# Loads of the first five units and of both weights, split in halves between the SP queue and the ScalarE queue

## The chip, the cores and the metric

One core of a Trainium2 chip runs the whole kernel. The metric is the device time of one execution in microseconds (us). On one core a single run's state is not marked by a second die, so runs more than 1.5% above the fastest of the same kernel are taken as slow and left out of the ratios. Times in the tables are medians; times of single instructions come from the profiled execution of each kernel, counted from the start of its span.

## The reference, cut to what matters

The program is a recurrent attention (a state of 48x48 per head that decays by w and takes in k times v), followed by a feed-forward block with a SoLU activation and a layer norm.

```python
def _attn_ref(r, k, v, w, u):            # batch 4, heads 8, sequence 768, head size 48
    for t in range(S):
        cur = einsum('bhd,bhe->bhde', u[None] * kt, vt)
        y[:, :, t] = einsum('bhd,bhde->bhe', rt, state + cur)
        state = wt[:, :, :, None] * state + einsum('bhd,bhe->bhde', kt, vt)

def _moe_ref(x, w_in, w_out, g_ln):      # 3072 tokens, 384 -> 1024 -> 384
    h = x @ w_in
    solu = h * softmax(h)                # [written out in the reference]
    return layernorm(solu) * g_ln @ w_out
```

All inputs and the output are float32.

## The kernel before

The work is cut into 24 units of 128 time steps of one batch. A unit needs four tensors, w, k, r and v, of 128 x 8 x 48 float32 (192 KB, 1,024 rows of 192 bytes). All loads are issued by SyncE, the SP queue. Those of units 0 to 4 and of both weights are asked for at the very start:

```python
    def load(i):
        c, b = units[i]
        for name, src in (("w", w), ("k", k), ("r", r), ("v", v)):
            t = io.tile([C, H, D], F32, tag=name + "_in", name=name + "_in")      # 6 buffers
            sp.dma_start(out=t, in_=src[b, :, c * C:(c + 1) * C, :].rearrange("h t d -> t h d"))
            live[i][name] = t

    # [u and g rows: two small loads from sp]
    load(0)
    win_f = consts.tile([128, KM, DF], F32)
    sp.dma_start(out=win_f, in_=moe_w_in.rearrange("(ko ki) f -> ki ko f", ki=128))
    load(1)
    # [w_out: two halves, both from sp]
    for i in range(2, 5):
        load(i)
```

ScalarE ("act") opens each unit with the logarithm of w; the running sums, the decays and all else hang on it:

```python
    def log_w(i):
        act.activation(out=L["lw"][:, :, :D], in_=L["w"], func=LN)
    def decays(i):
        act.activation(out=cum[:, :, :DM], in_=cum[:, :, :DM], func=EXP)
```

A fixed list of stages gives the order of instructions on every engine, and each engine keeps that order:

```python
ORDER = """
lw0 cum0 vb0 p0 win1 rows ubc exp0 q0 kp0 p1 rp0 lw1 cum1 dg0 win2 win0 exp1 kp1 krk1 ... gw3 M0 ...
lw2 ... lw3 ...
mean m2 mean_sb sel2 kp3 et0 H0 e0 p3 rp3 H1 Y2 lw4 q3 w2 he0 krk3 krr3 y2 Oa0 ...
"""                                                          # [cut]
```

The stages "win" cast w_in to bf16, "gw" scale w_out, "mean" and "w2" centre it, "H" is the first matmul of the feed-forward block, and "Oa0" is the first half of the output matmuls of unit 0.

The softmax here doesn't subtract the row's maximum and nothing guards it: scores larger than these inputs give would overflow.

## Time and profile before

| | before |
|---|---|
| device time, median of the first 3 runs | 170.99 us (169.93 to 172.01) |
| span of the profiled run | 169.6 us |
| TensorE, VectorE, ScalarE, GpSimd busy | 85%, 71%, 70%, 63% |
| first activation on ScalarE | 4.60 us |
| first output matmul | 37.30 us |
| loads of the start | 7.08 MB |

Read it as two stages. Until the first output matmul TensorE is idle for half of the time (18.8 of 37.3 us): it waits for data and for a string of short steps on the other engines. After it TensorE is almost never idle. The lines that show this stand in the prediction.

### The profile page before, as it was taken

How to read it: one execution, taken by the hardware profiler on the slowest of the kernel's cores; microseconds unless marked ns; L12 is line 12 of the kernel's file. 1: busy time of each engine (PE TensorE's matmuls, PEld its weight loads, DVE VectorE, ACT ScalarE, POOL GpSimd, SP SyncE). 2: the span in 40 equal slices, each digit the busy share in tenths (PEclk: the TensorE clock that was granted, in tenths of full speed). 3: DMA queues.
4: the chain of work that ended last, by engine and by line, in shares of the span. 5: the costliest groups of instructions: out<-in, count | busy, mean ns of one | idle time of the engine just before them, and what ended most of it. 6: DMA issues, size and time to landing. Idle time of an engine off the chain costs nothing.

```text
span 169.6 us, 5377 instructions
## 1 busy us (share of the span) xinstructions
PE 144.7 (85%) x2139; PEld 114.4 (67%) x2139; DVE 119.8 (71%) x280; ACT 118.2 (70%) x243; POOL 107.4 (63%) x157
## 2 busy tenths in 40 slices
PE   0503669939899999999999999999999999999980
PEld 0102336816788798878878887788877778798860
DVE  7017577796978779778988867697767988665440
ACT  3305395534869878888788968987878786767752
POOL 3225595824899886969989955779365629544000
PEclk9999999987999999999999999999999999999996
DMA  3999999999999999899999998999921011101212
GB/s 78 249 320 224 325 179 192 167 190 187 170 203 182 203 176 213 199 199 178 240 183 183 178 243 165 192 183 163 249 90 50 0 50 46 50 2 50 93 48 93
DMA packets 104795, 27.09 MB, mean 160 GB/s; under 512 B 100281, under 2 KB 104386, under 8 KB 104770
## 3 DMA queue, kind: packets, MB, share of 16 engines
q1 hardware_dynamic: 104770, 26.75, 79.7%
q8 instruction: 16, 0.26, 0.7%
q14 instruction: 9, 0.07, 0.1%
HBM read 22.03 MB, written 4.72 MB: 158 GB/s over the span
## 4 chain that ended last, share of the span: by engine, by line
PE 78%; DVE 6%; DMA 5%; ACT 3%; SPq 2%; POOL 2%; issue 2%; POOLq 0%; DVEq 0%
PE o_ps L63 22%; PE h_ps L63 18%; PE kr_ps L63 7%; PE g_ps L63 6%; PE y_ps L63 6%; PE m_ps L63 5%; PE s_ps L63 5%; DMA w_in<-in_w_dram 5%; PE cum_ps L63 4%; PE x_ps L63 3%; DVE w L63 3%; SPq L63 2%; POOL m L63 1%; DVE kr L63 1%; PE mean_ps L63 1%
## 5 line engine op out<-in xcount | busy, mean ns | idle before, releaser
L63 PE MATMUL o_ps<-w,he 128*128 128x385 bf16 x192 | 51.8, 330 | 2.9 <-DVE he L63 2.9
L63 PE MATMUL g_ps<-he 128*128 128x128 bf16 x192 | 42.3, 221 | 0.0
L63 POOL TENSOR_SCALAR_AFFINE_SELECT m<-m 128x1024 bf16<-128x1024 bf16 x24 | 26.4, 1101 | 18.9 <-ACT m L63 14.5
L63 PE MATMUL h_ps<-xT,win_sb 128*128 128x128 bf16 x576 | 35.9, 219 | 0.0
L63 PEld LDWEIGHTS <-win_sb 128*128 128x128 bf16 x576 | 32.8, 98 | 0.8 <-DVE xT L63 0.5
L63 PE MATMUL o_ps<-inv_col,e 128*128 128x1 bf16 x192 | 32.2, 168 | 0.0
L63 ACT ACTIVATE e<-h_ps 128x1024 bf16<-128x1024 f32 x24 | 24.5, 1022 | 9.8 <-PE h_ps L63 9.8
L63 DVE TENSOR_TENSOR he<-h_ps,e 128x1024 bf16<-128x1024 f32 x24 | 29.3, 1223 | 2.2 <-ACT e L63 1.3
L63 ACT CAST m<-m_ps 128x1024 bf16<-128x1024 f32 x24 | 24.3, 1012 | 8.9 <-PE m_ps L63 8.6
L63 PEld LDWEIGHTS <-he 128*128 128x128 bf16 x384 | 24.5, 97 | 4.9 <-DVE he L63 3.1
L63 PEld LDWEIGHTS <-e 128*128 128x128 bf16 x192 | 18.8, 98 | 13.3 <-issue 0.9
L63 POOL TENSOR_TENSOR dv<-vb,dg 128x384 bf16<-128x384 bf16 x24 | 19.8, 828 | 10.1 <-DVE dg L63 10.0
L63 POOL TENSOR_TENSOR q<-p,u_bc 128x384 bf16<-128x384 bf16 x24 | 21.8, 910 | 4.7 <-DVE gr L63 4.2
L63 POOL TENSOR_TENSOR p<-r_in,k_in 128x384 bf16<-128x384 f32 x24 | 24.1, 1003 | 1.0 <-DMA r_in<-in_r_dram 1.0
L63 DVE COPY kr<-kr_ps 128x1024 bf16<-128x1024 bf16 x24 | 16.5, 690 | 10.2 <-PE kr_ps L63 10.0
L63 ACT ACTIVATE cum_ps<-cum_ps 128x768 f32<-128x768 f32 x24 | 19.2, 801 | 5.2 <-PE cum_ps L63 3.0
L63 ACT ACTIVATE lw<-w_in 128x384 bf16<-128x384 f32 x23 | 12.0, 522 | 7.1 <-DMA w_in<-in_w_dram 7.1
L63 DVE TENSOR_TENSOR kp<-cum_ps,k_in 128x384 bf16<-128x384 f32 x24 | 13.4, 556 | 4.8 <-ACT cum_ps L63 4.0
L63 PEld LDWEIGHTS <-kr 64*128 64x128 bf16 (+1 forms) x272 | 11.5, 99 | 6.3 <-DVE kr L63 2.8
L63 POOL TENSOR_TENSOR qm<-ss,sq 128x1 f32<-128x1 f32 x24 | 4.5, 189 | 17.2 <-DVE junk L63 13.7
L63 DVE TENSOR_TENSOR st<-s_ps,et 64x192 bf16<-64x192 f32 x40 | 14.1, 352 | 1.6 <-ACT et L63 0.6
L63 ACT ACTIVATE o<-o_ps,rs 128x384 f32<-128x384 f32 x24 | 13.9, 579 | 0.3
(72 smaller groups left out, 253.4 us busy)
## 6 DMA issues: line engine op xcount, KB each, us to landing
w_in<-in_w_dram SPq DMA_DIRECT2D x24, 192.0 KB, 4.6
k_in<-in_k_dram SPq DMA_DIRECT2D x24, 192.0 KB, 4.6
r_in<-in_r_dram SPq DMA_DIRECT2D x24, 192.0 KB, 4.8
v_in<-in_v_dram SPq DMA_DIRECT2D x24, 192.0 KB, 4.8
out_dram<-o SPq DMA_DIRECT2D x24, 192.0 KB, 2.9
win_f<-in_moe_w_in_dram SPq DMA_DIRECT2D x1, 1536.0 KB, 8.1
wout_f<-in_moe_w_out_dram SPq DMA_DIRECT2D x2, 768.0 KB, 7.0
u_row<-in_u_dram SPq DMA_DIRECT2D x1, 1.5 KB
```

What stands on the lines that cost most here:

```text
L63: made = make(*args, **kwargs)
```

## The change

The intent is to have two queues ask for the data of the start. Each tensor of units 0 to 4, w_in and w_out becomes two halves, one from SP and one from ScalarE's queue. Units 5 to 23 stay whole and on SP.

```diff
         for name, src in (("w", w), ("k", k), ("r", r), ("v", v)):
             t = io.tile([C, H, D], F32, tag=name + "_in", name=name + "_in")
-            sp.dma_start(out=t, in_=src[b, :, c * C:(c + 1) * C, :].rearrange("h t d -> t h d"))
+            rows = src[b, :, c * C:(c + 1) * C, :].rearrange("h t d -> t h d")
+            if i < 5:
+                sp.dma_start(out=t[:, :H // 2, :], in_=rows[:, :H // 2, :])
+                act.dma_start(out=t[:, H // 2:, :], in_=rows[:, H // 2:, :])
+            else:
+                sp.dma_start(out=t, in_=rows)
@@
-    sp.dma_start(out=win_f, in_=moe_w_in.rearrange("(ko ki) f -> ki ko f", ki=128))
+    win_v = moe_w_in.rearrange("(ko ki) f -> ki ko f", ki=128)
+    for half, queue in enumerate((sp, act)):
+        part = slice(half * DF // 2, (half + 1) * DF // 2)
+        queue.dma_start(out=win_f[:, :, part], in_=win_v[:, :, part])
@@
-    for half in range(2):
+    for half, queue in enumerate((sp, act)):
         part = slice(half * KF // 2, (half + 1) * KF // 2)
-        sp.dma_start(out=wout_f[:, part, :], in_=wout_v[:, part, :])
+        queue.dma_start(out=wout_f[:, part, :], in_=wout_v[:, part, :])
```

## The prediction

> **What bounds the kernel now.** I began with the page's busy shares and its 40 slices (4.24 us each). TensorE is busy 85% of the span, the others 63 to 71%, and the slices show two stages. The last row is the mean busy share of the 16 DMA engines.
>
> ```profile
> PE   0503669939899999999999999999999999999980
> DMA  3999999999999999899999998999921011101212
> ```
>
> TensorE is nearly full from the ninth or tenth slice to the last but one; before that it is mostly idle. The DMA engines are full from the second slice to the 29th. The view of stretches puts numbers on it (columns: stretch, length, TensorE busy, instructions, granted clock, DMA share, GB/s):
>
> ```profile
> 0.00:37.30 37.30, 18.47 (x172) 1.00 1.02 215
> ...
> 40.00:165.00 125.00, 123.56 (x1947) 1.00 0.75 146
> ```
>
> From 40 to 165 us TensorE does 123.56 us of work in 125 us. Nothing but fewer or quicker matmuls shortens that stage. The other 37 us are the start, and any gain from loads must come from there: 18.47 us of TensorE work in 37.3 us, 18.8 us idle. The end of the start is in the chain of waits, in order of time (start, length, what):
>
> ```profile
> 31.42 4.69 DVE w L63 x8
> 36.11 1.14 DVE he L63
> 37.26 0.05 issue
> 37.30 0.50 PE o_ps L63
> ```
>
> At 37.30 the first output matmuls begin, and TensorE is dense from there. So the measure of the change is: when do these matmuls begin? The timeline of ScalarE shows what holds the start back now:
>
> ```profile
> 4.60 0.52 ACT L60 ACTIVATE lw<-w_in 128x384 bf16<-128x384 f32 x1 [2.51 <-DMA w_in<-in_w_dram]
> 6.00 0.80 ACT L63 ACTIVATE cum_ps<-cum_ps 128x768 f32<-128x768 f32 x1 [0.89 <-PE cum_ps L63]
> 13.34 0.52 ACT L63 ACTIVATE lw<-w_in 128x384 bf16<-128x384 f32 x1 [6.54 <-DMA w_in<-in_w_dram]
> ...
> 19.27 0.61 ACT L63 ACTIVATE gw<-wout_f,gr 128x384 bf16<-128x384 f32 x1 [3.73 <-DMA wout_f<-in_moe_w_out_dram]
> ```
>
> ScalarE works on unit 0 at 4.60 us, then waits 6.54 us for the data of unit 1, which queue behind the 1.5 MB of w_in. These are the waits that the change is aimed at. But they are waits for bytes, not for the queue that asks for them: in 0 to 37.3 us the DMA share is 1.02.
>
> The timeline of the SP queue shows the price of asking (start, length of the issue):
>
> ```profile
> 5.33 0.49 SPq L63 DMA_DIRECT2D w_in<-in_w_dram  x1
> 5.86 2.08 SPq L63 DMA_DIRECT2D k_in<-in_k_dram  x1
> 7.98 3.98 SPq L63 DMA_DIRECT2D r_in<-in_r_dram  x1
> ...
> 27.93 2.01 SPq L63 DMA_DIRECT2D r_in<-in_r_dram  x1
> 29.98 0.79 SPq L63 DMA_DIRECT2D v_in<-in_v_dram  x1
> ```
>
> An issue with room ahead of it takes about 0.4 to 0.5 us; the third one after w_in takes 3.98 us, because the transfers ahead have not drained. The last of the start's loads (v of unit 4) is issued only at 29.98 to 30.77 us. SP has nothing else to do, so this costs nothing today. That is the row to remember.
>
> **What the Trainium skill says.** "DMA: Bandwidth & Descriptors", section "Issuing engines are not separate DMA queues": DMAs begun by ScalarE and SyncE run on the same 16 DMA engines and interleave; several issuers save only the issue time. The trace agrees as far as it can: the share is 1.02 with one issuer. Same page, "Queues, rings and completion order": SP and ACT each own one row, with a ring on each engine. So I expect ACT to have its own depth ahead; no row of this trace shows ACT issuing. "Perfetto Trace Analysis", section "DMA Instruction — HWDGE (DVE, Sync)": the reported length runs from the semaphores being satisfied until the sequencer is free for its next instruction, and includes the wait for the shared descriptor generator. The SP rows agree: each issue starts 0.04 us after the last ended. "TensorE: Matmul & The Clock Gate", section "Architectural detail": ScalarE's queue is a strict FIFO. So an activation cannot pass a DMA issue written ahead of it.
>
> **The change part by part.**
> *Removed:* half the bytes of each of 20 unit loads and of w_in from SP. w_out already was two halves; its second one moves to ACT.
> *Added:* 22 issues on ACT (5 units x 4, one half each of w_in and w_out). The order of instructions of the changed kernel shows all 22 after the table load and ahead of the first activation (lw of unit 0). PE, VectorE and GpSimd keep their order and work. Bytes are the same: 20 x 196,608 + 2 x 1,572,864 = 7.08 MB.
>
> *When ACT is free.* v loads land a median 4.3 us after their issue starts (0 to 36 us), so today v of unit 4 lands at 29.98 + 4.3 = 34.3 us. With the engines already full I keep that time. Its issue ended at 30.77, so one queue can stand 34.3 - 30.77 = 3.5 us ahead of the data, some 3.4 tensors at about 1.03 us each. Two rings of that depth, drained evenly, hold twice that, 7.1 us: ACT's last issue ends at 34.3 - 7.1 = 27.2 us. If the depth is shared, at 30.8. I choose **27.5 us** for the first activation, against 4.60.
>
> *What follows it.* All first-unit data are there by then, so I lay the rows of the trace after t0 (start of the first activation). Today exp of unit 0 starts 1.40 after lw (6.00 - 4.60) and takes 0.80: t0+2.2. lw of unit 1 takes 0.52. TensorE's order puts the u and g transposes (1.65 + 0.27 us, ending about t0+3.2) ahead of unit 1's cumulation, 0.8 us: t0+4.0. Then exp of unit 1, 0.80, to t0+4.85, and VectorE, meanwhile through its copies, kp, rp and a reduction of unit 0, starts kp of unit 1 at about t0+5.2. Today that row starts at 15.58, and the output matmuls 21.7 us later (37.30). That stretch is a string of dependent short steps and the 4.69 us of w2 sums, so it moves nearly whole. What it loses is the wait for w_out: gw at 19.27 to 19.88 pushed the copy of m, whose matmuls were done at 19.05, to 19.79, 0.7 us. So the output matmuls start at t0 + 5.2 + 21.7 - 0.7 = t0 + 26.2 = 53.7 us, against 37.3: **16.4 us later**.
>
> *What comes back.* Nothing that I can see. TensorE has the same work left at that point and was 98.8% busy doing it (123.56 of 125). Loads from unit 5 on are SP's alone and run ahead of need: DMA is nearly idle after the 29th slice. The sum is 171.0 + 16.4 = **187.4 us**.
>
> **The rivals.**
> *ACT's issues do not block it* (it hands them off, or its ring is far deeper). The start would be bounded by bytes as before: lw of unit 0 maybe 0.3 us sooner, w_in at 12.3 us about the same. Time 170 to 171, the same. Against it: SP issues visibly stall up to 3.98 us, and ACT needs more than 20 issues, where one queue stood only 3.4 tensors ahead.
> *Two rings draw more bandwidth.* Unit loads run at some 180 GB/s while the stretch of 5 to 12 us with w_in in it reached 306, so 192-byte rows leave speed unused. If two rings gave a fifth more, the loads would land near 28 us, ACT be free at about 22, and the time be 171.0 + 22 - 11.1 = 182. For it: that 306. Against: the share is 1.0 already. To beat 171 ACT would have to be free by 11.1 us, which means nearly all 7.08 MB gone by then; impossible at these rates.
> *The depth is one for both, or the queues wait for each other's lock.* ACT free at 31: 171 + 31 - 11.1 = 191.
> *The delay is absorbed later.* It would need idle TensorE time after 37.3 us; there are 1.4 us in 125.
>
> **Range and chances.** Time = 171.0 + t0 - 11.1. t0 from 22 to 31.5 us gives 182 to 191.5, with half a us for the rest of the string on either side. Slower by over 2% needs only t0 above 14.5 us; the chance that it fails is that of the first rival, some 5%.
>
> **What would show it.** In ScalarE's timeline: no activation before some 27 us. In ACT's issues: 22 of them, the first few under 0.6 us, later ones stalled like SP's. Output matmuls near 53.7. DMA share about 1 with about 215 GB/s in the first 30 us, loads landing near 34. TensorE idle some 35 us before the dense stage, which stays as dense. It is wrong if an activation stands among the issues, if the loads land well before 30 us, or if the stretch from unit 1's kp to the output matmuls is not about 21 us.

## The result and the profile after

The changed kernel takes 188.31 us (median of 4 runs, 187.69 to 188.78), against 171.25 us before (4 runs, 169.93 to 172.01). The ratio is 1.1003, with a 95% interval of 1.0925 to 1.1081. Here and below a ratio is the mean time of one kernel's fast runs over that of the other's of the same rounds, so it is not quite the ratio of the medians quoted.

The two rows of the 40 slices, each now 4.64 us, in the page of the changed kernel:

```profile
PE   0000006579758999999999999999999999999990
DMA  6999999999830699699939899777960102101122
```

TensorE now does nothing in the first six slices. The DMA engines were full from the second slice, as before: the data came, and hardly anybody worked on them. In the view of stretches (stretch, length, then busy time of TensorE, its weight loads, VectorE, ScalarE and GpSimd, granted clock, DMA share, GB/s):

```profile
0.00:53.20 53.20, 17.09 (x173) 11.30 (x173) 22.98 (x68) 16.35 (x26) 19.21 (x32) 1.00 1.21 208
...
56.00:181.00 125.00, 123.69 (x1941) 101.09 (x1939) 95.29 (x207) 99.26 (x212) 87.35 (x123) 0.99 0.62 125
```

The start grew from 37.3 to 53.2 us with the same TensorE work in it (18.47 and 17.09 us, busy). The dense stage is as dense as it was: 123.69 us of 125, before 123.56. So nearly the whole difference lies ahead of the first output matmul: 15.9 us of the 16.1 by which the two profiled spans differ (169.6 and 185.7 us). The chain of waits, in order of time:

```profile
52.00 1.14 DVE he L63
53.14 0.05 issue
53.19 0.34 PE o_ps L63
```

These are the steps (after the sums of w2) that ended the start before as well, 15.9 us later. Why later is in ScalarE's timeline (start, length, engine, what; ACTq are its DMA issues):

```profile
0.83 0.43 ACTq L60 DMA_DIRECT2D w_in<-in_w_dram  x1
...
4.37 0.50 ACTq L63 DMA_DIRECT2D w_in<-in_w_dram  x1
...
11.71 0.37 ACTq L63 DMA_DIRECT2D wout_f<-in_moe_w_out_dram  x1
...
17.01 0.38 ACTq L63 DMA_DIRECT2D v_in<-in_v_dram  x1
...
23.04 0.37 ACTq L63 DMA_DIRECT2D v_in<-in_v_dram  x1
...
25.97 0.37 ACTq L63 DMA_DIRECT2D r_in<-in_r_dram  x1
27.03 0.38 ACTq L63 DMA_DIRECT2D v_in<-in_v_dram  x1
27.45 0.52 ACT L63 ACTIVATE lw<-w_in 128x384 bf16<-128x384 f32 x1 [25.36 <-DMA r_in<-in_r_dram]
```

The first activation starts at 27.45 us, 0.04 us after the 22nd issue ended. Its own operand, w of unit 0, was complete by 4.7 us. (The releaser in brackets is inferred from a counter that r of unit 4 had taken over by then. In the runs e2 to e6 below, all with issues on ScalarE ahead of the first activation, this follows the last of them by 0.04 or 0.05 us, whatever the bracket names.) And the issues are not long: the 22 records last 0.37 to 0.53 us and sum to 8.94 us, of the 26.6 us from the first to the last. The other 17.6 us lie between them. The view of waits names engines and, of the queues, SP's alone; SP's issues of the start have the same gaps. Waits of the SP queue, 0 to 34 us (total, times, longest):

```profile
SPq L63 <- DMA win_f<-in_moe_w_in_dram: 3.7, 1, 3.7
SPq L63 <- DMA v_in<-in_v_dram: 3.6, 3, 2.6
```

and the same kernel's chain of waits, early part:

```profile
12.07 5.47 DMA v_in<-in_v_dram
17.54 0.02 issue
17.55 6.07 DMA r_in<-in_r_dram
```

An issue waits until an earlier transfer has landed, and a later issue waits for that one in turn. Before the change SP waited for no landing in the whole start. The instructions of the built program say which wait it is, for ScalarE's issues too. They name eight completion counters that all transfers of a program use in turn, whichever queue issues them (not a profile; the digit after HW names the counter):

```
 5 L63 DMACopy v_in_84<-in_v_dram 128x4x48 [waits DMAHW1_49]
 6 L63 DMACopy win_f_87<-in_moe_w_in_dram 128x3x512 [waits DMAHW3_49]
 7 L63 DMACopy w_in_90<-in_w_dram 128x4x48 [waits DMAHW5_49]
 8 L63 DMACopy k_in_93<-in_k_dram 128x4x48 [waits DMAHW7_49]
 9 L63 DMACopy r_in_96<-in_r_dram 128x4x48 [waits DMAHW1_49]
```

ScalarE's halves have the odd counters and SP's the even ones, so each half waits for the landing of the fourth half before it on its own queue. Eight halves in flight are 768 KB, four tensors.

The records of the trace bear this out, for ScalarE too: they hold the counter of each issue and the time of each landing, though no view prints them together. The rows at 4.37, 11.71, 17.01, 23.04 and 27.03 us above are one chain. The half of w of unit 1 landed at 11.69 us, and the half of w_out began at 11.71; it landed at 16.99, and v of unit 2 began at 17.01; that landed at 23.02, and v of unit 3 began at 23.04; that landed at 27.01, and v of unit 4, the last issue, began at 27.03. So this chain of landings sets the start of the first activation. The kernel before has the same eight counters, but there a counter means a whole tensor: the queue was full (some 3.4 tensors, by the prediction's estimate, which is on the high side, as shown below) before the counters ran out, and the wait was inside the issues, up to 3.98 us in one. The prediction had not looked at these waits.

### The profile page after: what moved, and what is told of

Read it like the earlier page. It is cut to its first block, busy times and chain, and to the rows that moved or that the text cites. A ratio compares the mean times of both kernels' runs of the same rounds, so it can differ in the third digit from the quotient of the medians.

```text
span 185.7 us, 5417 instructions
## 1 busy us (share of the span) xinstructions
PE 143.6 (77%) x2139; PEld 114.2 (61%) x2139; DVE 121.3 (65%) x280; ACT 118.0 (64%) x243; POOL 107.6 (58%) x157
## 3 DMA queue, kind: packets, MB, share of 16 engines
q1 hardware_dynamic: 94002, 23.21, 66.6%
## 4 chain that ended last, share of the span: by engine, by line
PE 68%; DMA 14%; DVE 5%; issue 4%; POOL 3%; ACT 3%; SPq 0%; POOLq 0%; DVEq 0%
PE o_ps L63 20%; PE h_ps L63 16%; PE g_ps L63 6%; PE y_ps L63 6%; PE kr_ps L63 6%; DMA r_in<-in_r_dram 5%; PE s_ps L63 4%; DMA win_f<-in_moe_w_in_dram 4%; PE m_ps L63 4%; PE cum_ps L63 3%; DMA v_in<-in_v_dram 3%; DVE w L63 3%; PE x_ps L63 2%; DMA w_in<-in_w_dram 2%; POOL m L63 1%
## 5 line engine op out<-in xcount | busy, mean ns | idle before, releaser
L63 POOL TENSOR_SCALAR_AFFINE_SELECT m<-m 128x1024 bf16<-128x1024 bf16 x24 | 26.4, 1099 | 17.6 <-ACT m L63 13.2
L63 PE MATMUL h_ps<-xT,win_sb 128*128 128x128 bf16 x576 | 35.9, 219 | 0.1
L63 ACT ACTIVATE lw<-w_in 128x384 bf16<-128x384 f32 x24 | 12.5, 522 | 25.4 <-DMA r_in<-in_r_dram 25.4
L60 PE MATMUL cum_ps<-lw,uti_neg 128*128 128x384 bf16 x1 | 0.5, 477 | 28.0 <-ACT lw L63 28.0
L63 PEld LDWEIGHTS <-uts 128*128 128x128 bf16 x24 | 2.5, 103 | 27.4 <-issue 27.3
```

The lines of the kernel that those rows point to most:

```text
L60: made = make(*args, **kwargs)
L63: made = make(*args, **kwargs)
```

## The experiments

Nine kernels ran, all correct. "t0" is the start of the first activation, "Oa0" the start of the first output matmul in the profiled run. The ratio is to the kernel before in the same rounds, whose medians were 171.25, 171.78 (e1 to e4), 170.69 (e5 to e7) and 171.54 us (e8, e9). One run of e8 and two of e9 count as slow; they are in the medians and not in the ratios.

| run | ScalarE issues ahead of its first activation | t0 | Oa0 | median us | ratio (95%) |
|---|---|---|---|---|---|
| before | 0 | 4.60 | 37.3 | 171.25 | |
| the change | 22 halves | 27.45 | 53.2 | 188.31 | 1.1003 (1.0925 to 1.1081) |
| e1 halves, all SP | 0 | 4.53 | 37.8 | 172.78 | 1.0078 (1.0017 to 1.0139) |
| e2 units 0, 1, w_in | 9 halves | 9.68 | 36.3 | 171.63 | 0.9998 (0.9948 to 1.0049) |
| e3 units 0 to 2, weights | 14 halves | 17.60 | 43.6 | 178.72 | 1.0406 (1.0346 to 1.0467) |
| e4 whole tensors | 12 whole or half weights | 29.45 | 55.3 | 190.05 | 1.1034 (1.0941 to 1.1126) |
| e5 tiny loads | 22 of 4 KB | 16.29 | 42.1 | 176.35 | 1.0296 (1.0221 to 1.0371) |
| e6 issues later | 9, then 13 in between | 9.86 | 46.4 | 181.39 | 1.0579 (1.0504 to 1.0654) |
| e7 unit 1 before w_in | 0 | 4.54 | 36.6 | 169.96 | 0.9938 (0.9844 to 1.0032) |
| e8 w_in earlier | 0 | 4.67 | 35.9 | 169.68 | 0.9869 (0.9831 to 0.9907) |
| e9 two ScalarE issues | 2 whole | 4.00 | 31.9 | 169.87 | 0.9867 (0.9816 to 0.9918) |

### e1: the same halves, none from ScalarE

```diff
-                act.dma_start(out=t[:, H // 2:, :], in_=rows[:, H // 2:, :])
+                sp.dma_start(out=t[:, H // 2:, :], in_=rows[:, H // 2:, :])
# and (sp, act) -> (sp, sp) for both weights
```

> The same halves, all 44 of them from the SP queue, none from ScalarE. Theory (ScalarE's strict order: its activations stand behind its 22 issues): no activation is held, the first at about 4.6 us, output matmuls near 37, time 169.5 to 172.5, as before. Rival (halving itself costs: more transfers, more landings to wait for): most of the loss stays, 178 us or more.

172.78 us: of the 10% loss, 0.8% stays. Halving is not what costs; the queue is. With the same halves and counters, but one queue, SP waited for no landing in the first 34 us: its waits were inside the issues, up to 1.80 us for one half. The 172.78 is a little above the range, and the profile has a reason to offer: an issue of a half takes about 0.53 us, two of them no less than one whole, and unit 1's first activation came at 14.50 us, before at 13.34.

### e2 and e3: fewer units on ScalarE

```diff
-            if i < 5:
+            if i < 2:          # e2, with both halves of w_out from sp;  e3: i < 3
```

> ScalarE issues only the halves of units 0 and 1 and of w_in, 9 issues. In the changed kernel its 9th issue ended at 9.55 us. Theory (time = 160.9 + start of the first activation, once that is later than the waits that bound the start anyway, about 10.4 us): first activation near 9.6, and because unit 1's data come only at 13.3 the delay is swallowed: 170 to 172.5 us. Rival (each us that ScalarE stands costs a us): 171.2 + (9.6 - 4.6) = 176 us.

> ScalarE issues the halves of units 0 to 2 and of both weights, 14 issues; in the changed kernel the 14th ended at 17.4 us. Theory: first activation at 17 to 18 us, time 160.9 + 17.4 = 178.3 (177 to 180). Rival (each us costs a us from 4.6 on): 184.

In e2 ScalarE's timeline reads:

```profile
9.26 0.37 ACTq L63 DMA_DIRECT2D v_in<-in_v_dram  x1
9.68 0.52 ACT L63 ACTIVATE lw<-w_in 128x384 bf16<-128x384 f32 x1 [7.59 <-DMA w_in<-in_w_dram]
...
13.12 0.52 ACT L63 ACTIVATE lw<-w_in 128x384 bf16<-128x384 f32 x1 [1.24 <-DMA w_in<-in_w_dram]
```

The first activation is 5.1 us later than before, and the time is the same: unit 1's data arrive only at 13.1 us, and ScalarE still waits 1.24 us for them. The delay fits in a wait that was there. In e3 ScalarE is held to 17.60 us, past that wait, and the time is 178.72, expected 178.3. Both rivals (176 and 184) fall. So a late ScalarE costs one for one, but only beyond some 10 us (an estimate: 171.0 less the 160.9 us that follow the first activation in the changed kernel; no run lies between 9.68 and 16.29).

### e4: whole tensors, half of them from ScalarE

```diff
+            queue = act if i < 5 and n % 2 else sp        # n: 0 w, 1 k, 2 r, 3 v
-            sp.dma_start(out=t, in_=src[...])
+            queue.dma_start(out=t, in_=src[...])
# w_in whole from act; w_out: one half from each
```

> No halves: for units 0 to 4 w and r whole from SP, k and v whole from ScalarE, w_in whole and half of w_out from ScalarE; 12 issues on ScalarE, each twice as large. This tells what sets how far the issues run ahead of the data. Theory A (the eight completion semaphores that all DMAs share in turn: in the changed kernel eight halves, 768 KB, are the most in flight; here it would be eight whole ones): ScalarE can run further ahead, first activation at 24 to 26 us if the rings of the two queues are separate and hold 3.4 tensors each, time 185 to 187, and the long waits are inside the issues. Theory B (one depth of 3.4 tensors for both queues): first activation at 28 to 30, time 189 to 191. If the landing of data alone mattered: as the changed kernel, 27.5 and 188.3.

190.05 us and t0 = 29.45. The numbers are those of theory B, but the profile does not show one depth for both queues. ScalarE's timeline:

```profile
11.09 0.44 ACTq L63 DMA_DIRECT2D wout_f<-in_moe_w_out_dram  x1
20.40 0.37 ACTq L63 DMA_DIRECT2D k_in<-in_k_dram  x1
...
27.36 2.05 ACTq L63 DMA_DIRECT2D v_in<-in_v_dram  x1
29.45 0.52 ACT L63 ACTIVATE lw<-w_in 128x384 bf16<-128x384 f32 x1 [27.36 <-DMA w_in<-in_w_dram]
```

Two kinds of wait stand here. From 11.53 to 20.40 us ScalarE's queue stands between two issues: by the trace's records the second one waits for the counter of a load that SP had issued, w of unit 2, which landed at 20.38. So an issue on one queue is held by a transfer of the other. SP meanwhile ran ahead and had issued its whole share of the start by 22.04 us, so ScalarE's share came last. Then, at the end, the wait is inside the issues, 2.05 us each, as in the kernel before but at half its rate, while SP's issues at 28.35 and 30.53 us took 2.06 and 2.05 us too. Both queues are full then and drain evenly. ScalarE's last tensor landed 7.8 us after its issue began, at 35.2, that is 5.75 us after it ended: at 2.05 us a tensor, 2.8 tensors ahead on ScalarE's own queue. So the two queues do have separate depths, as theory A held, and A's time still failed, because of the counters and of the unequal progress. The run does not tell what the depth alone would have made of the changed kernel.

### e5: the issues without the bytes

```diff
+    tiny = consts.tile([128, 22, 8], F32)
+    def small_load():                      # 22 times, where the change has its halves
+        act.dma_start(out=tiny[:, n, :], in_=moe_w_in[0:128, n * 8:n * 8 + 8])
# all real loads as in the kernel before, whole, from sp
```

> The kernel before (all real loads whole, from SP), with 22 loads of 4 KB each added on ScalarE's queue ahead of its first activation, read by nobody. It measures the issues without the bytes. Theory (an issue waits for the landing of the transfer eight places earlier among all transfers, because eight completion counters are used in turn): in this program's order one of the last small loads has its counter from w_in, which lands near 12.3 us, so ScalarE is held until then plus some four more issues of 0.4 us: first activation near 14 us, output matmuls 25.9 later at 39.9, time 175 (173.5 to 176.5). Rival 1 (only the issues cost, 22 x 0.4 us, free at about 10): 170 to 172. Rival 2 (22 issues hold ScalarE for as long as the loads run, whatever they carry): 185 or more.

```profile
1.24 15.00 ACTq L63 DMA_DIRECT2D tiny<-in_moe_w_in_dram  x21
16.29 0.52 ACT L63 ACTIVATE lw<-w_in 128x384 bf16<-128x384 f32 x1 [14.20 <-DMA w_in<-in_w_dram]
```

90 KB of loads that nobody reads hold ScalarE to 16.29 us and cost 3%. If only the issues counted, whose records sum to 9.9 us, it would have been free near 11. The time, 176.35, is in the range of the counter theory (173.5 to 176.5), but its t0 of 14 was 2.3 us too early, and the wait was not quite the one that I had reckoned: small loads that stand beside w_in land late themselves. SP's queue, which also has to wait for them here, shows that:

```profile
SPq L63 <- DMA tiny<-in_moe_w_in_dram: 10.0, 5, 6.9
```

SP stood 6.9 us for one load of 4 KB, and issued unit 1's w at 13.64 us, before at 5.33. So it is shown that issues wait for landings across queues, and that they do so even where ScalarE's own loads carry next to no bytes. By the trace's records ScalarE stood from 3.21 to 4.68 us for SP's w of unit 0 (landed at 4.66), and from 11.24 to 13.27 us for its own small load of 6.78 us, issued just behind w_in (landed at 13.24). The 3% is not the price of ScalarE's hold alone: unit 1's data were late too, so that even a free ScalarE could not have begun unit 1 at 13.34 us, as before.

### e6: the issues between the activations

```diff
+    flush_after = {"exp1": 2, "exp2": 3, "exp3": 4}   # unit whose ScalarE halves are issued there
# half of w_out goes with unit 2
```

> All 22 halves stay on ScalarE's queue, but only 9 (units 0, 1, w_in) ahead of its first activation; half of w_out and those of unit 2 stand after the exponential of unit 1, those of unit 3 after that of unit 2, those of unit 4 after that of unit 3. Theory (what costs is that activations stand behind issues that wait): first activation near 9.7 us, then waits of a few us in all in the middle of the start: 172 to 178 us. Rival (22 halves on a second queue cost what they cost wherever they stand, by slower transfers): 186 to 190.

181.39 us, between the two, outside the range of my theory. The reason is in ScalarE's timeline:

```profile
14.79 0.43 ACTq L63 DMA_DIRECT2D wout_f<-in_moe_w_out_dram  x1
19.93 0.37 ACTq L63 DMA_DIRECT2D w_in<-in_w_dram  x1
...
25.17 0.37 ACTq L63 DMA_DIRECT2D v_in<-in_v_dram  x1
25.59 0.61 ACT L63 ACTIVATE gw<-wout_f,gr 128x384 bf16<-128x384 f32 x1 [10.02 <-DMA k_in<-in_k_dram]
```

Five issues between two activations still held ScalarE for 10 us, on the path. By the trace's records the two long gaps ended when loads of the other queue landed: SP's half of k of unit 2 at 19.91 us and of v at 23.21. The same queue, the same 22 halves: moving them gained 6.9 us of the 17. What costs is where the wait stands, but I had thought of it as "a few us" and did not count the counters in the middle.

### e7, e8 and e9: what the change was after

In the kernel before, unit 1 waits because w_in (1.5 MB) is asked for ahead of it, though w_in is used only at 30.7 us. These runs move w_in back instead of adding a queue.

```diff
     load(0)
-    sp.dma_start(out=win_f, ...)
     load(1)
     # w_out
-    for i in range(2, 5): load(i)
+    load(2); load(3); sp.dma_start(out=win_f, ...); load(4)       # e7
+    # e8: only the w of unit 3 ahead of w_in;  w2 ahead of kp3 in ORDER
+    # e9: as e8, with w and k of unit 0 from act
# casts of w_in moved to just ahead of H0, two on ScalarE and one on GpSimd
```

> Not the change, but the wait it aimed at: all loads whole and from SP, with w_in moved from behind unit 0 to behind unit 3, and its three casts moved to just ahead of the matmuls that use them. Theory (the start is bound by bytes in the order asked for): unit 1's first tensor lands near 8.7 us, not 13.3; w_in near 28.5, its casts by 30.5; output matmuls near 34 instead of 37.3, time 168 to 170. Rival (the start is bound by its string of steps or by w_in itself): 171 or more.

> The run with unit 1 ahead of w_in (e7), in which w_in landed at 29.67 us and became the bound (output matmuls at 36.6). Here w_in goes four tensors earlier, behind only the w of unit 3, and the sums of w2 stand ahead of unit 3's products on VectorE. Theory (bytes in the order asked for): w_in lands near 26.7 us, casts by 28.7, output matmuls near 33.2 to 34; with the 135 us that follow them in every run so far, 168 to 169 us. Rival (unit 3's late k and r hold VectorE and ScalarE): no better than e7's 170.

> e8, with the w and k of unit 0 whole from ScalarE's queue and all else from SP: 2 issues on ScalarE, both before it has anything to do (they would end by 1.9 us, while its table load runs to 2.1 us). Theory (issues cost nothing where ScalarE has nothing to do and no counter to wait for): w lands at about 3.9 instead of 4.55 us, all later loads 0.5 us sooner, time 0.3 to 0.8 us under e8. Rival (any issue on ScalarE costs): above e8 by the two issues, 0.9 us.

In e7 unit 1's first activation came at 8.96 us, not 13.34, as expected. But w_in landed at 29.67 us, its casts ended at 31.68, the first matmuls on it took 4.22 us for 46 of them (before 2.84 for 48; the granted clock was 0.67 from 31.7 to 36.6 us, before 1.00 from 30 to 35), and the output matmuls began at 36.6, not near 34. The wait was exchanged for another, and the time is the same: 0.9938 with 1 in the interval. e8 is 1.3% under the kernel before, with the interval below 1; its 169.68 us misses my 168 to 169. w_in came as reckoned (its casts ran from 26.6 to 28.6 us), but the output matmuls began at 35.9, not at 33.2 to 34. e9 shows no gain over e8 in time, though its two issues cost nothing (its first activation is 0.67 us earlier) and its output matmuls begin at 31.9. How much of these 4 us against e8 is due to the two issues is not shown: in e8 the granted clock was 0.66 from 26 to 36 us and one first matmul on w_in took a median 311 ns, in e9 1.00 from 24 to 32 us and 219 ns; no run here says why. Its chain of waits shows why:

```profile
34.20 5.21 DMA w_in<-in_w_dram
39.44 0.52 ACT lw L63
```

Here the dense stage has a hole: the work has overtaken the data. The "135 us after the output matmuls begin" that held in the other runs (133.4 to 135.3, the median less Oa0) is 138.0 here. The best of these versions, e8 and e9, are 1.3% under the kernel before, and so well under the changed one.

## Why the prediction was right or wrong

**The bound.** Right. The dense stage did not change, and the first output matmul is the mark that decides.

**ScalarE's order.** Right, and it is the cause: no activation stood among the 22 issues, and with the same halves on SP (e1) the loss is nearly gone. e3 and e5 give sizes in between, on one line: Oa0 less t0 is 25.7 us in the change, 26.0 in e3, 25.8 in e4 and e5; the prediction put it at 26.2. The stretch from unit 1's kp (32.55 us) to the output matmuls is 20.6 us, predicted about 21.

**When ScalarE is free.** The number, 27.5 against 27.45, is nearly exact, and the step to it failed: "Two rings of that depth, drained evenly, hold twice that, 7.1 us". Both of its terms were off, and they cancelled. The loads landed by 32.3 us (the last SP half, issued at 28.60, took 3.7 us), not 34.3. (34.3 was a median laid onto the last load; by its counter's increments in the trace of the kernel before, that load landed at about 33.8, which makes the depth there 3.1 us, 2.9 tensors, close to the 2.8 of e4. And "the engines already full" did not hold to the end: their share was 0.35 from 29.9 to 30.7 us.) And ScalarE stood 4.9 us ahead of that, not 7.1: with halves, the eight shared counters let no more than four tensors' worth be in flight. That the counters set this depth rests on the waits and landings in the trace, the built program, and the gaps between short issues; no run had more counters. The last issue ended at 27.41 = 32.3 - 4.9. That the two errors cancelled is luck.

**The form of the stall.** Wrong. "Later ones stalled like SP's": no issue lasted more than 0.53 us. The wait stood between the records, as the section "DMA Instruction — HWDGE (DVE, Sync)", which the prediction cites, says of an issue's record (it begins once its semaphores are satisfied), and I did not draw the conclusion that a queue can stall without one long record.

**The sum.** The output matmuls were put at 53.7 and came at 53.19. The time was put at 187.4 and came to 188.31; the dense stage and the tail took 135.1 us after the output matmuls in place of the 133.7 that I carried over from before (171.0 - 37.3).

**The rivals.** Two rings did not draw a fifth more: 225 GB/s in the first 34 us, before 217. The delay was not absorbed later. The first rival, that the issues do not block, is refuted. The rival of one depth for both queues (ScalarE free at 31 us, time 191) fails by its number, though a part of it holds: the eight counters are one limit for both queues.

## What to carry to other kernels

A second DMA queue on a compute engine is not free: its issues stand in that engine's order, and each may wait for a landing. Before giving a compute engine loads to issue, count those that stand ahead of its first useful instruction and ask for each what it waits for: a full queue, or a completion counter that it shares with other transfers; the second does not show as a long issue but as a gap. If the data engines are already full, change the order of the bytes and not the number of askers (worth 1.3% here), and expect the next-latest transfer or step to become the wait.

## What the Trainium skill lacked or had wrong

- "DMA: Bandwidth & Descriptors", section "Issuing engines are not separate DMA queues", says that issuing from several engines only saves issue time. It agrees on bandwidth (217 and 225 GB/s), but lacks that it can cost the second issuer its own work: ScalarE was held to 27.45 us, and the kernel lost 10%.
- No page that I used gives how far a queue can run ahead of its data. For these 192 KB transfers of 192-byte rows the run with whole tensors shows 2.8 tensors on ScalarE's own queue; separate queues, as the section "Queues, rings and completion order" of the same page says, with both draining at 2.05 us a tensor.
- The same page says of completion semaphores that each transfer in flight needs its own. It does not say what follows where a program has only eight for all: 22 loads of 4 KB held ScalarE to 16.29 us.
- "Perfetto Trace Analysis", section "DMA Instruction — HWDGE (DVE, Sync)", agrees with the runs, but does not say in so many words that a queue's stall can be invisible in the lengths of its records: 8.94 us of records in 26.6 us.
